# Running maxima from score copies in SBUF, GpSimd's arithmetic on VectorE, and new tables of rounds in a gated mix of attention and a gated FFN

## The chip, the core and the metric

The kernel runs on one core of one Trainium2 chip. The metric is the device time of one execution in microseconds (us); a program's time is the median over its runs. The core's engines run side by side, each through its own instructions in order: TensorE (PE, with its weight loads as PEld), VectorE (DVE), ScalarE (ACT), GpSimd (POOL) and SyncE (SP, which here only issues DMAs). They wait for each other through semaphores. SBUF is the working memory of 128 partitions, PSUM holds the outputs of matmuls.

## What is computed

```python
def _A_ref(x, wqkv, wo):                       # 16 heads of 28, 2048 tokens, D = 448
    qkv = (x @ wqkv).reshape(B, S, 3, H, Dh).transpose(2, 0, 3, 1, 4)
    q, k, v = qkv[0], qkv[1], qkv[2]
    scores = jnp.einsum("bhqd,bhkd->bhqk", q, k) * (Dh ** -0.5)
    p = _softmax(scores, axis=-1)
    o = jnp.einsum("bhqk,bhkd->bhqd", p, v)
    return o.transpose(0, 2, 1, 3).reshape(B, S, D) @ wo

def _B_ref(x, W_gate, W_up, W_down):           # F = 1792
    gate = x @ W_gate
    up = x @ W_up
    gate = gate * (gate > 0)
    return (gate * up) @ W_down

g = _sigmoid((A_x * gate_w).sum(-1, keepdims=True))
out = g * _A_ref(A_x, A_wqkv, A_wo) + (1 - g) * _B_ref(A_x, B_W_gate, B_W_up, B_W_down)
```

## The kernel before

**Precision.** Operands of the projections and of the FFN are split into a high part (ScalarE's copy to a rounded type, `act_high`) and a low part (the difference, `low` on VectorE or `pool_low` on GpSimd), and each product is a sum of 11 terms (`TERMS`) over chunks of 128 rows.

**Three stages.** First come the projections of Q, K and V, whose results go to DRAM (`qk_d`) through GpSimd's DMA queue. Then come 32 rounds, two for each head. Last come the rest of the gate/up units, the down projection and the output projection. The change lies in the rounds and at the border to them.

**One round.** Round `v` works on head `v // 2` and half of the keys. A "visit" has 16 pairs of score matmuls (`score`, K against Q, 128 keys x 512 queries twice, into one PSUM tile of 1024 columns). 12 of the 16 pairs go through ScalarE's exp straight into the probability tiles `P` (`done`): for the first three blocks of queries the maximum is already folded into the matmul through two extra rows of Q. The four pairs of the last block of queries are raw: ScalarE copies them to SBUF (L262), VectorE keeps a running maximum (`block_max`, L228, tile `rm`) that reads them in PSUM, GpSimd reduces it over the partitions (`all_max`, L234), VectorE subtracts it from 2048 columns at a time (`take_max`, L239), and ScalarE takes the exp (`take_exp`, L246). A round's second half rescales the head's sum where the maximum of its two visits differs (`rescale`). At the end of a round the PV product (`pv`, tile `po`, L601) runs as 64 matmuls in two halves without a pause.

Beside the scores a round holds 12 pairs of "maxima" matmuls (`smax`, tile `sm`, L169), which compute the next heads' row maxima for the folded rows; VectorE reduces each pair (L171), and `smax_end` turns them over and stores them into Q's extra rows. And it holds the gate/up matmuls of the FFN (`gu_mm`, L547), 11 for each half of a unit of 128 hidden columns; `relu` and `spill_h` take them away, and a DMA stores them. In the first rounds ScalarE and GpSimd also split the gate/up weights (`split_f`, L103 and L112), 14 units in all, which then go to DRAM and are loaded again for later token blocks.

**What sets the order.** No scheduler: each engine's order is the order in which the code records instructions, and the four strings `FIRST`, `LONG`, `WIDE` and `LATE` set it within a round. One letter is one step: `s` a pair of scores, `m` a pair of maxima with its reduction, `x` one gate/up matmul, `A` the all-reduce, `d` a subtraction, `e` an exp of 2048 columns, `n` the end of a head's maxima, `w` the split of weights, `c` and `f` the rescaling, `P` and `Q` the halves of the PV product, `u` and `l` leftovers of the projections. `LONG` has 33 `x`, `WIDE` 44, `LATE` no `m`. `AHEAD = 3` of a visit's pairs are issued in the round before. Score pairs and maxima pairs take turns in three PSUM tiles (`ps_w`): a pair waits until the pair three before it has been read. `small_things` issues a head's loads and the division by the row sums at the start of a round and at its eighth `s`: at the start of an even round `load_k` and `load_q` for two heads on, at the eighth `s` `row_sums` and `spread` (a reciprocal, its store, and four loads back that wait for the store).

## Time and profile before

| | us |
|---|---|
| median of 3 runs | 1289.12 (1284.76 to 1290.27) |
| the profiled execution: time | 1281.88 |
| the profiled execution: span of its trace | 1280.1 |
| busy in the span: PE, PEld | 1241.6 (97%), 872.5 (68%) |
| busy in the span: DVE, ACT, POOL | 962.1 (75%), 776.1 (61%), 191.2 (15%) |

Ends of matmuls are modelled and overlap with the next ones, so PE's 97% is no measure of how well it is used; the times from one PV block to the next are. In a row of the trace the columns are start, duration, engine, line, operation, output<-inputs, shape and count, and in brackets the idle time before it with the engine that ended it. `PEclk` is the granted clock of TensorE (1.00 is full speed).

### The profile page before, as it was taken

How to read it: one execution, taken by the hardware profiler on the slowest of the kernel's cores; microseconds unless marked ns; L12 is line 12 of the kernel's file. 1: busy time of each engine (PE TensorE's matmuls, PEld its weight loads, DVE VectorE, ACT ScalarE, POOL GpSimd, SP SyncE). 2: the span in 40 equal slices, each digit the busy share in tenths (PEclk: the TensorE clock that was granted, in tenths of full speed). 3: DMA queues.
4: the chain of work that ended last, by engine and by line, in shares of the span. 5: the costliest groups of instructions: out<-in, count | busy, mean ns of one | idle time of the engine just before them, and what ended most of it. 6: DMA issues, size and time to landing. Idle time of an engine off the chain costs nothing.

```text
span 1280.1 us, 16867 instructions
## 1 busy us (share of the span) xinstructions
PE 1241.6 (97%) x6431; PEld 872.5 (68%) x6431; DVE 962.1 (75%) x1022; ACT 776.1 (61%) x894; POOL 191.2 (15%) x188
## 2 busy tenths in 40 slices
PE   9999699999999999999999999999999999999998
PEld 6888466665656666666666566666666566799998
DVE  6466679898988989998988889898989543563342
ACT  5223377777877677777777677767777784122121
POOL 4222221221221000000000001000000010551020
PEclk9999899999999999999999999999999999999999
DMA  9845275352626543342536243342442325745432
GB/s 323 289 189 222 84 209 117 127 163 72 169 76 201 169 121 84 103 133 64 163 104 186 81 113 103 84 130 93 132 128 76 119 90 195 228 147 159 132 115 80
DMA packets 64269, 178.37 MB, mean 139 GB/s; under 512 B 13730, under 2 KB 20578, under 8 KB 59554
## 3 DMA queue, kind: packets, MB, share of 16 engines
q1 hardware_dynamic: 57452, 151.00, 39.5%
q0 software_dynamic: 6304, 25.82, 5.3%
q8 instruction: 51, 0.84, 0.3%
q10 hardware_dynamic: 432, 0.46, 0.1%
q14 instruction: 30, 0.25, 0.1%
HBM read 118.58 MB, written 58.87 MB: 139 GB/s over the span
## 4 chain that ended last, share of the span: by engine, by line
PE 89%; DVE 4%; ACT 2%; DMA 2%; issue 1%; POOL 1%; SPq 0%; POOLq 0%; ACTq 0%
PE gu L547 19%; PE s L256 19%; PE po L601 18%; PE sm L169 13%; PE acc L808 10%; PE qk L381 5%; DVE rm L228 3%; PE wo L767 3%; PE v L399 3%; ACT P L262 1%; DVE mx L171 1%; DMA wg<-ws_d 1%; DMA or<-o_d 0%; DMA wr<-wq 0%; ACT P L260 0%
## 5 line engine op out<-in xcount | busy, mean ns | idle before, releaser
L171 DVE TENSOR_REDUCE mx<-sm 128x1 f32<-128x1024 f32 x384 | 456.5, 1219 | 60.6 <-PE sm L169 59.5
L547 PE MATMUL gu<-X,wg 128*128 128x512 f32 x1232 | 373.9, 398 | 10.8 <-POOL wg L112 7.2
L260 ACT ACTIVATE P<-s 128x1024 f32<-128x1024 f32 x306 | 306.7, 1025 | 116.8 <-PE s L256 113.1
L256 PE MATMUL s<-Q,K 128*128 128x512 f32 x1024 | 319.5, 403 | 13.6 <-DVE rm L228 11.2
L547 PEld LDWEIGHTS gu<-X,wg 128*128 128x128 f32 x1232 | 231.6, 189 | 69.1 <-POOL wg L112 7.6
L256 PEld LDWEIGHTS s<-Q,K 128*128 128x128 f32 x1024 | 184.7, 189 | 99.3 <-DVE rm L228 10.9
L169 PE MATMUL sm<-K,Q 128*128 128x512 f32 x768 | 243.2, 398 | 7.5 <-DVE mx L171 3.6
L601 PE MATMUL po<-P,V 128*32 128x512 f32 x1640 | 227.3, 594 | 0.0
L228 DVE TENSOR_TENSOR rm<-s,rm 128x512 f32<-128x512 f32 x218 | 150.4, 690 | 74.6 <-ACT P L262 57.3
L169 PEld LDWEIGHTS sm<-K,Q 128*128 128x128 f32 x768 | 137.1, 188 | 52.6 <-ACT P L260 10.1
L234 POOL PARTITION_ALL_REDUCE rm<-rm x32 | 57.2, 1788 | 673.7 <-DVE rm L228 618.8
L601 PEld LDWEIGHTS po<-P,V 128*32 128x32 f32 x1640 | 62.6, 110 | 116.2 <-issue 111.5
L808 PE MATMUL acc<-WD,hh 128*128 128x448 f32 x672 | 138.5, 365 | 0.0
L262 ACT ACTIVATE P<-s 128x1024 f32<-128x1024 f32 x104 | 105.1, 1024 | 46.6 <-PE s L256 45.4
L808 PEld LDWEIGHTS acc<-WD,hh 128*128 128x128 f32 x672 | 126.2, 188 | 10.4
L239 DVE TENSOR_TENSOR P<-P,rm 128x2048 f32<-128x2048 f32 x52 | 117.9, 2272 | 5.8 <-POOL rm L234 5.8
L601 PE MATMUL po<-V 128*32 128x512 f32 x408 | 115.0, 594 | 0.0
L103 ACT ACTIVATE hh<-hr 128x512 fp32r<-128x512 f32 x56 | 35.2, 631 | 117.8 <-PE acc L808 113.8
L246 ACT ACTIVATE P<-P 128x2048 f32<-128x2048 f32 x52 | 99.4, 1914 | 5.3 <-DVE P L239 4.5
L260 ACT ACTIVATE V<-s 128x1024 f32<-128x1024 f32 x78 | 78.9, 1025 | 37.1 <-PE s L256 35.2
L109 DVE TENSOR_TENSOR hh<-hr,hh 128x512 fp32r<-128x512 f32 x56 | 49.4, 883 | 62.2 <-ACT hh L103 62.2
L381 PE MATMUL qk<-X,W 128*128 128x512 f32 x308 | 77.4, 398 | 0.3 <-DVE X L109 0.2
(79 smaller groups left out, 772.4 us busy)
## 6 DMA issues: line engine op xcount, KB each, us to landing
wg<-ws_d SPq DMA_DIRECT2D x42, 896.0 KB
K<-qk_d SPq DMA_DIRECT2D x64, 224.0 KB
Q<-qk_d SPq DMA_DIRECT2D x64, 224.0 KB
h_d<-h SPq DMA_DIRECT2D x56, 256.0 KB
hr<-h_d SPq DMA_DIRECT2D x56, 256.0 KB
ws_d<-wg SPq DMA_DIRECT2D x14, 896.0 KB
qk_d<-st POOLq DMA_DIRECT2D x21, 512.0 KB, 3.2
wgr<-wgu SPq DMA_DIRECT2D x13, 512.0 KB
```

Of the source, the lines that this page charges most:

```text
L169: nc.tensor.matmul(ps[:, c, :], Q[h][:, u * P:(u + 1) * P], K[h % 3][:, k0:k0 + TB], start=True, stop=True)
L171: nc.vector.tensor_reduce(MX[h][:, 2 * u + half:2 * u + half + 1], ps, axis=AX.XY, op=OP.max)
L228: nc.vector.tensor_tensor(r, x, y, op=OP.max)
L239: nc.vector.tensor_tensor(QUAD[q], QUAD[q], RM[v, b].unsqueeze(1).to_broadcast([P, 4, TB]), op=OP.subtract)
L246: nc.scalar.activation(q, q, AF.Exp, scale=SCALE)
L256: nc.tensor.matmul(ps[:, c], K[h % 3][:, k * P:(k + 1) * P], Q[h][:, j * TB:(j + 1) * TB], start=True, stop=True)
L260: nc.scalar.activation(dst, ps, AF.Exp, scale=SCALE)
L262: nc.scalar.activation(dst, ps, AF.Copy)
L381: nc.tensor.matmul(ps, W[:, a, c * P:(c + 1) * P], xf(tb, b), start=(n == 0), stop=(n == NT - 1))
L547: nc.tensor.matmul(ps, WS[i][:, s, a], xf(i // NF, b), start=(n == 0), stop=(n == NT - 1))
L601: nc.tensor.matmul(po[32 * j:32 * j + 32], V[:, h // 4 % 2, k, h % 4], AT.pop((v, k, j)), start=(k == k0), stop=(k == k0 + NK // 2 - 1))
L808: nc.tensor.matmul(ACC[i // NF][t][:, :D], HH[i][:, a, t * P:(t + 1) * P], WD[:, f, b], start=(f == 0 and n == 0), stop=(f == NF - 1 and n ...
```

## The change

- `block_max` becomes `block_min` on a step of its own, `b`: ScalarE copies a raw pair to SBUF with its sign turned, and VectorE takes the minimum of whole pairs (128x1024, both inputs in SBUF) into a tile `r2`: three such operations a visit, then one minimum of its two halves and one turn of the sign (with the maximum of the earlier visit, in the second half), both 128x512. No instruction but ScalarE's copy reads a raw pair in PSUM.
- `take_max` adds the negated maximum on VectorE (step `g`); the exp gets a negative scale. A way by DMA (step `d`) stands in the code, but no string has the letter.
- The low parts of the gate/up weights go from GpSimd to VectorE in all 28 halves.
- `AHEAD = 4`: all four raw pairs are issued in the round before.
- A first all-reduce of a small tile stands right at the program's start.
- `load_k` and `load_q` move behind `row_sums` and `spread`, and these from a round's eighth `s` to its tenth. The zero rows of the third Q buffer come by DMA from another Q buffer, not from a GpSimd memset.
- New strings, with the same counts of `m` and `x` (`FIRST` has one `s` more), and `WIDE` at other rounds.

```diff
-AHEAD = 3
+AHEAD = 4
-FIRST = "AmxmxsmxmxxlxsxumsmmmxxxsxdxxxsxssmxxmxsmmxdexxsxsewsPQ"
-LONG = "ssmnAxxxxsmsxmxsmxxxmsmxxxsmxxmxsdxsxxxsxsmxxxsmxxmexxsmxxdxxcsxsefwsPQ"
+FIRST = "mmbslmxusbssmsxbxsxmxxsmxxmmsxxsxsAxgbxsmsbxxxxmmxegmxxbxxPweQ"
+LONG = "AnsmsxxxxsxxssxgmxxxxsmsxxsxssgxmxsxxmsmxxxmsmxxxxscmxsxemxxxbxxsmxbmbPefwQ"
...
-        if k % (NK // 2):
-            parts = [(p[:, c], r) for c in range(2)]
-        elif v % 2:
-            parts = [(p[:, 0], RM[v - 1, b]), (p[:, 1], r)]
-        else:
-            parts = [(p[:, 0], q[:, 1])]
-        for x, y in parts:
-            nc.vector.tensor_tensor(r, x, y, op=OP.max)
...
+        if (v, b) not in R2:
+            R2[v, b] = att.tile([P, 2, TB], F32, name=f"r2_{v}_{b}", tag="r2", bufs=1)
+            left[v, b] = NK // 4 - 2
+            nc.vector.tensor_tensor(R2[v, b], todo_max.pop(0)[2], todo_max.pop(0)[2], op=OP.min)
+            return
+        nc.vector.tensor_tensor(R2[v, b], R2[v, b], todo_max.pop(0)[2], op=OP.min)
...
+        nc.vector.tensor_tensor(r, r2[:, 0], r2[:, 1], op=OP.min)
+        if v % 2:
+            nc.vector.scalar_tensor_tensor(r, r, -1.0, RM[v - 1, b], op0=OP.mult, op1=OP.max)
+        else:
+            nc.vector.tensor_scalar(r, r, -1.0, None, op0=OP.mult)
...
-        nc.vector.tensor_tensor(QUAD[q], QUAD[q], RM[v, b].unsqueeze(1).to_broadcast([P, 4, TB]), op=OP.subtract)
+            nc.vector.tensor_tensor(QUAD[q], QUAD[q], m, op=OP.add)
...
-            nc.scalar.activation(dst, ps, AF.Copy)
+            nc.scalar.activation(dst, ps, AF.Copy, scale=-1.0)
+            todo_max.append((v, chunks[0][1], dst))
...
+        nc.gpsimd.partition_all_reduce(warm_r, warm_r, P, bass_isa.ReduceOp.max)
...
-        if q == 0 and h and h + 2 < H:
-            load_k(h + 2)
-            load_q(h + 2)
...
             row_sums(h - 1)
             spread(h - 1)
+            if h + 2 < H:
+                load_k(h + 2)
+                load_q(h + 2)
...
-                if ns == 8:
+                if ns == 10:
                     small_things(2 * v + 1)
...
-                    split_f(parts // 2, act_high, pool_low, (parts % 2,))
+                    split_f(parts // 2, act_high, low, (parts % 2,))
...
-                nc.gpsimd.memset(f32(QS[2])[96:128], 0.0)
+                for a, b in ((GD, 12), (GD + 12, 4)):
+                    nc.sync.dma_start(f32(QS[2])[a:a + b].rearrange("p j t -> p (j t)"), Q[1][GD + 2:GD + 2 + b].bitcast(F32))
```

Three places show how the order of instructions moves. VectorE around the end of a round in the second half of the rounds, before the change (`sm` are maxima pairs, `s` score pairs in PSUM, `os` the head's output):

```order
L228 TENSOR_TENSOR rm_6653<-s_8_3_6649,rm_6653 128x512
L228 TENSOR_TENSOR rm_6653<-s_10_3_6659,rm_6653 128x512 x2
L228 TENSOR_TENSOR rm_6653<-s_12_3_6666,rm_6653 128x512 x2
L627 TENSOR_TENSOR os_6235<-os_6235,rb_6571 128x512
L228 TENSOR_TENSOR rm_6653<-s_14_3_6712,rm_6653 128x512 x2
L171 TENSOR_REDUCE mx_6722<-sm_6723 128x1
```

And the end of an early round with the change (`r` is the tile of pairwise minima, `wg` the split weights):

```order
L222 TENSOR_TENSOR r_3_0_1794<-r_3_0_1794,V 128x1024
L228 TENSOR_TENSOR rm_0_1820<-r_3_0_1794 128x512
L230 SCALAR_TENSOR_TENSOR rm_0_1820<-rm_0_1820,rm_0_1574 128x512
L109 TENSOR_TENSOR wg_1841<-wgr_1367,wg_1841 128x384 x2
L109 TENSOR_TENSOR wg_1841<-wgr_1367,wg_1841 64x2x128
L109 TENSOR_TENSOR wg_1852<-wgr_1606,wg_1852 128x384 x2
L109 TENSOR_TENSOR wg_1852<-wgr_1606,wg_1852 64x2x128
L634 TENSOR_TENSOR os_1386<-os_1386,rb_1705 128x512
L109 TENSOR_TENSOR mh_1897<-mr_1896,mh_1897 16x128
L171 TENSOR_REDUCE mx_1911<-sm_1912 128x1
```

The maximum of a round's last raw pair stood between the output and the next round's first reduction; now the whole chain is closed before the round's end, and in early rounds two units of weights follow it.

GpSimd at its first all-reduce of the rounds, before the change (`ISA` without operands loads code for the next operation; `pair` holds the first unit's raw weights):

```order
L112 TENSOR_TENSOR wg_1145<-pair,wg_1145 128x384
L234 ISA
L234 ISA rm_1150<-rm_1150 128x512
L388 DMA qk_d<-pair 128x2x512
L112 ISA
L112 TENSOR_TENSOR wg_1145<-pair,wg_1145 128x384
L112 TENSOR_TENSOR wg_1145<-pair,wg_1145 64x2x128
L716 MEMSET Q_1200 32x2048
```

With the change:

```order
L411 DMA v_d_79<-V 128x512
L392 DMA qk_d<-pair 128x2x512
L238 ISA rm_0_1218<-rm_0_1218 128x512
L175 MEMSET m_1315 128x4
L238 ISA rm_0_1321<-rm_0_1321 128x512
```

The low parts, the memset of Q and both loads of code are gone from this place; a load of code stands at the program's start.

SP's queue over an even round, before the change (`ls` and `l_d` are the row sums, `rb` their spread, `h_d` a stored hidden tile):

```order
L611 DMA ls_6471<-os_6235 128x1x16
L148 DMA K_103<-qk_d 28x2048 x4
L153 DMA Q_106<-Q_106 2x2048
L155 DMA Q_106<-qk_d 28x2048 x4
L617 DMA l_d_90<-rq_6568 128x16
L623 DMA rb_6571<-l_d_90 32x512 x4
```

With the change:

```order
L618 DMA ls_6461<-os_6230 128x1x16
L573 DMA h_d_6510<-h_6508 128x512
L546 DMA wg_6512<-ws_d_2367 128x1792
L624 DMA l_d_90<-rq_6540 128x16
L630 DMA rb_6543<-l_d_90 32x512 x4
L148 DMA K_103<-qk_d 28x2048 x4
L153 DMA Q_106<-Q_106 2x2048
L155 DMA Q_106<-qk_d 28x2048 x4
```

The eight loads of K and Q pass from the head of the round to behind the store of the reciprocal and the four loads that wait for it.

More of the change, by code (lines that the diff above doesn't have):

```diff
@@ L245, in take_exp, with score @@
         q = QUAD[q].rearrange("p c t -> p (c t)")
-        nc.scalar.activation(q, q, AF.Exp, scale=SCALE)
-    def score(late=True):
+        nc.scalar.activation(q, q, AF.Exp, scale=-SCALE)
+    def score():
         v, done, q, half, chunks = stream.pop(0)
@@ L423, in gated_mix_kernel @@
         nc.vector.memset(warm, 0.0)
+        warm_r = pa.tile([P, 16], F32, name="warm_r")
+        nc.vector.memset(warm_r, 0.0)
         ps = ps_x("warm_ps")
@@ L495, in gated_mix_kernel @@
                 m += 1
-            news = [(score, False) for back in EARLY if back == len(mixed) - n]
+            news = [(score,) for back in EARLY if back == len(mixed) - n]
             for k, c in enumerate(news):
@@ L654, in small_things @@
             spread(h - 1)
+            if h + 2 < H:
+                load_k(h + 2)
+                load_q(h + 2)
         if h and q == 2:
             normalise(h - 1)
-    split_f(0, act_high, pool_low, (0,))
+    split_f(0, act_high, low, (0,))
     fetch_f(1)
-    while todo_max:
-        block_max(*todo_max.pop(0))
     for v, (order, nu) in enumerate(ROUNDS):
@@ L722, in gated_mix_kernel @@
                 pv(v, "PQ".index(o))
-        left = [k for k in todo_exp + todo_sub + todo_all if k[0] == v]
-        assert not passes and not left and v not in PO or len(stream) == max(0, 16 * (2 * H - 1 - v) - AHEAD), (v, passes, left, len(stream) + 16 * (v + 1))
+        rest = [k for k in todo_exp + todo_sub + todo_all if k[0] == v]
+        assert not passes and not rest and v not in PO or len(stream) == max(0, 16 * (2 * H - 1 - v) - AHEAD), (v, passes, rest, len(stream) + 16 * (v + 1))
     assert not stream and m == len(maxima), (len(stream), m)
```

49 lines of the change are left out of this document (25 added, 24 removed).

## The prediction

> **What bounds the kernel now.** I read the shares of the chain of waits first, then the busy time by stretches, then the chain in order of time, then the rows around two places where TensorE stops.
>
> ```profile
> PE 89%; DVE 4%; ACT 2%; DMA 2%; issue 1%; POOL 1%; SPq 0%; POOLq 0%; ACTq 0%
> ...
> 128.00:160.00 32.00, 20.50 (x72) 14.36 (x71) 21.87 (x21) 10.37 (x16) 9.20 (x10) 0.84 0.23 84
> 192.00:320.00 128.00, 125.50 (x678) 81.15 (x680) 113.85 (x114) 99.40 (x113) 24.45 (x24) 1.00 0.42 120
> 832.00:960.00 128.00, 126.19 (x669) 82.97 (x668) 114.26 (x116) 92.69 (x95) 7.22 (x6) 1.00 0.41 121
> ```
>
> TensorE holds 89% of the chain. In the stretches (columns: length, PE, PEld, DVE, ACT, POOL busy, clock) it is busy 125 to 126 us of 128, and VectorE 114 of 128: the rounds run close to both. Only 128 to 160 us, where the first round starts, is loose: 20.5 us of 32 and a granted clock of 0.84.
>
> ```profile
> 318.29 7.00 PE po L601 x64
> 344.68 0.94 PE gu L547 x4
> 347.23 7.00 PE po L601 x64
> ```
>
> A LONG round lasts 347.23 - 318.29 = 28.94 us. Its work: 16 score pairs, 12 maxima pairs and 33 gate/up matmuls are 89 matmuls at 0.94/4 = 0.235 us, 20.9 us, plus the PV block, 7.0 us: 27.9. About 1.0 us of a round is lost, and this is where:
>
> ```profile
> 325.23 1.20 PE L256 MATMUL s<-Q,K 128*128 128x512 f32 x4
> 326.69 0.70 PE L169 MATMUL sm<-K,Q 128*128 128x512 f32 x2 [0.27 <-DVE rm L228]
> 326.92 1.02 ACT L260 ACTIVATE P<-s 128x1024 f32<-128x1024 f32 x1
> 327.06 1.41 DVE L228 TENSOR_TENSOR rm<-s,rm 128x512 f32<-128x512 f32 x2
> 327.24 1.10 PE L547 MATMUL gu<-X,wg 128*128 128x512 f32 x4
> 328.62 0.70 PE L256 MATMUL s<-Q,K 128*128 128x512 f32 x2 [0.28 <-DVE rm L228]
> 329.15 0.62 PE L169 MATMUL sm<-K,Q 128*128 128x512 f32 x2
> 347.16 5.36 PE L601 MATMUL po<-P,V 128*32 128x512 f32 x48
> ```
>
> From 325.23 to 329.15 twelve matmuls, worth 2.82 us, take 3.92: 1.1 lost. From there to 347.16 it is 77 matmuls in 18.0 us, worth 18.1: nothing lost. Both stops wait for the running maximum on VectorE, which reads the scores out of PSUM and so holds one of the three PSUM tiles past ScalarE's copy. That is the whole loss of a steady round, and the most that a steady round can win.
>
> ```profile
> 135.48 0.63 PE L256 MATMUL s<-Q,K 128*128 128x512 f32 x2
> 136.40 5.02 DVE L228 TENSOR_TENSOR rm<-P,rm 128x512 f32<-128x512 f32 x6
> 137.06 0.51 ACT L103 ACTIVATE wg<-pair 128x384 fp32r<-128x384 f32 x1
> 142.61 1.07 PE L169 MATMUL sm<-K,Q 128*128 128x512 f32 x2 [3.32 <-DVE mx L171]
> 144.76 1.48 PE L547 MATMUL gu<-X,wg 128*128 128x512 f32 x3
> 156.04 1.78 POOL L112 TENSOR_TENSOR wg<-pair,wg 128x384 fp32r<-128x384 f32 x2 [8.01 <-issue]
> 157.87 0.79 PE L547 MATMUL gu<-X,wg 128*128 128x512 f32 x1 [7.18 <-POOL wg L112]
> 170.32 7.24 PE po L601 x64
> ```
>
> The first round stops twice: 3.32 us behind seven maxima in a row on VectorE, 7.18 us behind a low part on GpSimd, which itself stands 8.01 us without a visible wait after GpSimd's first all-reduce. After each, TensorE is slow: three matmuls take 1.48 us.
>
> **The change, part by part.** VectorE's prices:
>
> ```profile
> L171 DVE TENSOR_REDUCE mx<-sm 128x1 f32<-128x1024 f32 x384 | 456.5, 1219 | 60.6 <-PE sm L169 59.5
> L228 DVE TENSOR_TENSOR rm<-s,rm 128x512 f32<-128x512 f32 x218 | 150.4, 690 | 74.6 <-ACT P L262 57.3
> L239 DVE TENSOR_TENSOR P<-P,rm 128x2048 f32<-128x2048 f32 x52 | 117.9, 2272 | 5.8 <-POOL rm L234 5.8
> L246 ACT ACTIVATE P<-P 128x2048 f32<-128x2048 f32 x52 | 99.4, 1914 | 5.3 <-DVE P L239 4.5
> L627 DVE TENSOR_TENSOR os<-os,rb 128x512 f32<-128x512 f32 x16 | 11.6, 724 | 0.0
> L109 DVE TENSOR_TENSOR X<-xr,X 128x1024 fp32r<-128x1024 f32 x6 | 7.3, 1224 | 3.6 <-ACT X L103 3.5
> L109 DVE TENSOR_TENSOR W<-wr,W 128x336 fp32r<-128x336 f32 x6 | 2.8, 504 | 2.0 <-ACT W L103 1.9
> L109 DVE TENSOR_TENSOR W<-wr,W 64x224 fp32r<-64x224 f32 x2 | 0.8, 390 | 0.1
> ```
>
> *Running maxima from SBUF.* Per visit out go 7 or 8 operations of 0.69 (5.2 us on the mean), in come three of 128x1024 and two of 128x512: 3 x 1.224 + 2 x 0.724 = 5.1. VectorE gains nothing; what is gained is that a raw score's PSUM tile is free after ScalarE's 1.02 us. I walked a new LONG round by hand: 0.47 us a pair on PE, 1.02 a copy or exp, 1.22 a reduction, three tiles in turn, 0.2 us from producer to consumer as between the rows above. Its start "s m s xxxx s xx s s" runs without a stop if VectorE is free within 2.0 us of the PV block's end (the fifth pair, wanted at 3.3, needs the first reduction done). The later stops are small, 0.2 to 0.3 each behind the second subtraction, 0.5 in all. So 1.1 lost becomes 0.5: **-0.6 a round, -17 over 28 LONG and WIDE rounds**. Bounds: -1.1 (nothing lost, -31) and 0 (the loss only moves).
>
> *Subtraction at later places.* Still two of 2.27 a round; adding the negated maximum costs what subtracting did. Both exps follow early enough: in the walk the second subtraction ends near 10.5 us, the PV block starts at 21.5, its second half at 25. Nothing.
>
> *Low parts on VectorE.* Fourteen units at 2 x 0.55 (384 elements, between the rows of 336 and 512) plus 0.4 for the 64-row tail (256 elements, the row of 224): 1.5 a unit, 21 us. They stand at the ends of the first eight rounds, one or two units each, behind the last minimum. VectorE ends that chain about when PV ends in the walk, so one unit plus the 0.7 of the output sum puts the next round's start 2.0 to 2.6 late, two units 3.5 to 4.1. Past 2.0 the fifth pair waits: 0.35, 0.7, 0.4, 0.9, 0.35, 2.2, 0.35, 0.8 over the eight boundaries, **+6**. Bounds: 0 (back-to-back operations overlap, as 1.41 for two of 0.69 does not yet show) and +12 (every unit in full over the 28.9 us rounds, less the 1 us of slack each has).
>
> A rule against just this: the Trainium skill's Perfetto Trace Analysis, under Optimizing Scalar/DVE Operations, says that GpSimd and VectorE share an SBUF read port, so that shifting work between them may not help. By it some of the 21 us was already paid as waiting, and the term would be nearer 0 than 6; no row here separates the two.
>
> *First round.* In GpSimd's order no low part follows an all-reduce any more, and a first all-reduce is done at the very start, so the 8.01 us has no place here. VectorE then sets this round. Before the second PV half it owes 11 reductions (13.4), the first visit's five operations (5.1), two minima of the next (2.45), two subtractions (4.54), the first unit's low parts, the last projection's low part and the gates (1.5 + 0.69 + 0.6), after 1.6 us of waiting for ScalarE's first high part (137.57): 29.85; then an exp, 2.1 with its hand-over, and half a PV block, 3.5: 35.5 us from 135.95, where the last score pair of the projections ends. Now it ends at 177.56, 41.6 us after: **-6**. Bounds: -9 (overlap) and -2 (VectorE idles 4 us between tiles).
>
> The clock belongs to this term: 0.84 in the first round's stretch, with matmuls at twice their time after stops of 3.32 and 7.18 us. My longest new stops are 2.2 and 2.5. The Trainium skill's TensorE: Matmul & The Clock Gate, Part 1, puts the halving after an idle window of about 3.4 us; the trace agrees, with its two stops. By that rule the new stops leave the clock alone; were both to halve it, an estimate from that page's 3.4 us is 2 x 1.7 us more.
>
> *The all-reduce at the start* pushes GpSimd's memsets and its first store of projections back by up to some 10 us, the 8.01 and the operation itself; three staging tiles and two halves of K's third buffer take five stores before a reuse, so 0 to +1. *The zero rows of Q by DMA* wait for VectorE's low part, where a GpSimd memset stood behind the 8.01 us: nothing. *Four pairs ahead* moves one pair from a round's start into the round before: in the walk above.
>
> *Loads of K and Q in mid round.* They pass from the head of an even round to behind the row sums' round trip on SP; the first user is the second matmul pair of the next round.
>
> ```profile
> 330.25 2.71 SPq L148 DMA_DIRECT2D K<-qk_d  x4
> 339.82 0.35 SPq L617 DMA_DIRECT2D l_d<-rq  x1
> 348.15 2.69 SPq L623 DMA_DIRECT2D rb<-l_d  x4
> 346.00:348.00 2.00, 2.00 (x14) 0.96 (x16) 2.00 (x2) 1.89 (x3) 0.00 (x0) 1.00 0.09 26
> 561.46 1.72 SPq L148 DMA_DIRECT2D K<-qk_d  x4
> 570.00:572.00 2.00, 2.00 (x10) 1.60 (x10) 2.00 (x3) 1.03 (x1) 0.00 (x0) 1.00 0.80 172
> 573.55 0.32 SPq L617 DMA_DIRECT2D l_d<-rq  x1
> 576.89 1.71 SPq L623 DMA_DIRECT2D rb<-l_d  x4
> ```
>
> K and Q took from 561.46 to about 572 with the queues busy, 10.5 us. New: the reciprocal at some 9.2 us into the round, 3.3 to the spread's issue, 1.7 for it, then 10.5: landed at 25, wanted at 29. Nothing, with 4 us to spare; queued behind it are the hidden tile's store and the next weights, wanted a round later.
>
> **Sum.** -17 + 6 - 6 = -17 us: a span of 1263 against 1280.1, 1265 against the profiled execution's own 1281.88. That execution lies below the three runs shown (1284.76 to 1290.27); against their median, 1289.12, the forecast is **1272**, its own range 1258 to 1281.
>
> **Rivals.**
> (1) *Only the first round wins.* The 1.1 us moves to the dense stretch "s m s m" after the second subtraction. For it: VectorE is busy 114 of 128 now and gets no relief. Against: the old rounds, as dense, lose nothing after 329.15. 1289 - 6 = 1283.
> (2) *Slower: VectorE becomes the bound.* Place: the round's end, where three minima, two 512s and the last reductions stand in one piece. If VectorE comes to the first reduction later than 2.0 us after PV in every round, not in eight, each round stops there. At 3.3 us the stop is 1.3, and with 0.5 within the round the loss is 1.8 against 1.1: +0.7 x 28 = +20, with -6 from the first round 1303. For it: an odd round carries four more 512-element operations (rescaling, normalising, output sum), 2.9 us at 0.724; with 12 reductions, two subtractions and the 5.1 that is 27.1 before the hidden products, in a round of 28. Against: it ends its chain before PV's end in my walk.
> (3) *Slower: K and Q land late.* The old spread waited 8.3 us (339.82 to 348.15) in a round with weight stores in the queue. With that and a slow drain (K issued at 330.25, the queues busy until 346) they land at 36, 7 us after their first use. In rounds 2, 4, 6 and 8: +28, and some 6 for a slowed clock: 1289 - 17 + 34 = 1306; in all thirteen loads over 1360. Against: the 8.3 us was spent behind K and Q themselves, which now come after.
>
> **Chances.** Forecast 0.60, (1) 0.14, (2) 0.16, (3) 0.10. The range, 1257 to 1300, holds the forecast, rival (1) and most of what (2) can cost. Half a per cent, 6.4 us, is about what can be told from no change: the forecast lies beyond it but for 0.03, half of (1) does, and 0.02 of each of (2) and (3) ends within it. Faster 0.61, same 0.17, slower 0.22.
>
> **What would show it.** Right: PV block to PV block 28.3 to 28.5 us in the second half and no wait of TensorE's scores for running maxima; the first PV block ending near 171 us with a clock above 0.84 before it; some longer rounds before 430 us. Wrong: rounds of 29 us or more after 450 us with waits for mx (rival 2), waits of sm for K or Q at the head of odd rounds (rival 3), or an idle GpSimd of 8 us still in the first round.

## The result, and the profile after

The changed kernel takes 1270.32 us (median of 4 runs, 1269.59 to 1270.41), the kernel before 1287.33 in the runs beside it: a ratio of 0.9866, 95% interval 0.984 to 0.9891. The forecast was 1272. The span of the profiled execution is 1268.6 us, against 1280.1 before.

The shares of the chain of waits and the busy time by stretches (length, PE, PEld, DVE, ACT, POOL busy, clock, DMA share, GB/s) of the changed kernel, as they were shown of the kernel before:

```profile
PE 86%; DVE 6%; ACT 3%; DMA 3%; issue 1%; POOL 1%; SPq 0%; ACTq 0%; DVEq 0%; POOLq 0%
...
128.00:160.00 32.00, 25.44 (x98) 16.94 (x96) 24.88 (x28) 21.58 (x28) 4.39 (x6) 1.00 0.61 168
192.00:320.00 128.00, 124.93 (x697) 77.72 (x697) 122.93 (x125) 96.24 (x115) 9.74 (x7) 1.00 0.40 120
320.00:448.00 128.00, 124.30 (x660) 80.50 (x659) 118.24 (x118) 93.11 (x103) 9.36 (x8) 1.00 0.46 146
832.00:960.00 128.00, 128.00 (x713) 80.39 (x713) 116.35 (x110) 92.00 (x97) 10.87 (x8) 1.00 0.39 113
960.00:1088.00 128.00, 119.41 (x636) 78.64 (x635) 59.55 (x64) 76.14 (x83) 11.49 (x7) 0.97 0.41 138
```

Two of these stretches in the kernel before:

```profile
320.00:448.00 128.00, 125.55 (x693) 79.09 (x686) 114.94 (x120) 94.81 (x107) 23.61 (x23) 1.00 0.52 154
960.00:1088.00 128.00, 125.87 (x702) 80.42 (x700) 74.47 (x85) 90.48 (x95) 10.19 (x8) 1.00 0.36 120
```

Four stages went four ways. The first round gained 5 us of TensorE's time in 128:160 and kept its clock at 1.00. The late rounds are full: 128.00 of 128. The early ones, 192 to 448, are no fuller than before, with VectorE now at 122.93 of 128. And 960:1088, which held 125.87 us before, holds 119.41 at a lower clock: something new is lost there.

Where a round begins and ends is read off TensorE's timeline, from the end of one PV block to the end of the next. By that, with the rounds numbered from 0:

| stretch | before, us | after, us | difference |
|---|---|---|---|
| to the end of the first PV block | 177.56 | 171.28 | -6.3 |
| rounds 1 to 8 (one WIDE more after) | 234.46 | 240.21 | +5.7 |
| rounds 9 to 28 (one WIDE fewer after) | 587.18 | 569.39 | -17.8 |
| rounds 29 to 31 (LATE) | 74.50 | 81.98 | +7.5 |
| rest | 206.40 | 205.74 | -0.7 |
| span | 1280.1 | 1268.6 | -11.5 |

A WIDE round is 2.1 to 2.3 us longer than a LONG one, so at equal work the early rounds lost 3.4 and the later ones won 15.6: the changed kernel's LONG rounds from 9 on last 28.21 to 28.28 us each. The start of one of them on PE and DVE, after a PV block that ends at 526.77:

```profile
526.74 0.71 PE L264 MATMUL s<-Q,K 128*128 128x512 f32 x2
527.29 0.63 PE L169 MATMUL sm<-K,Q 128*128 128x512 f32 x2
527.76 0.62 PE L264 MATMUL s<-Q,K 128*128 128x512 f32 x2
527.96 0.28 DVE L109 TENSOR_TENSOR mh<-mr,mh 16x128 fp32r<-16x128 f32 x1 [1.78 <-ACT mh L185]
528.17 1.21 DVE L171 TENSOR_REDUCE mx<-sm 128x1 f32<-128x1024 f32 x1
...
529.15 0.62 PE L264 MATMUL s<-Q,K 128*128 128x512 f32 x2
529.30 2.27 DVE L247 TENSOR_TENSOR P<-P,rm 128x2048 f32<-128x2048 f32 x1
...
530.08 1.09 PE L264 MATMUL s<-Q,K 128*128 128x512 f32 x4
```

No row of PE carries a wait in brackets. VectorE waits 1.78 us for ScalarE's copy of the transposed maxima, makes their low part and begins its reductions (528.17); no maximum of raw scores stands ahead of them. An early round, number 4, starts otherwise:

```profile
259.02 2.20 POOL L238 PARTITION_ALL_REDUCE rm<-rm  x1 [28.36 <-DVE rm L232]
259.60 3.72 DVE L109 TENSOR_TENSOR wg<-wgr,wg 128x384 fp32r<-128x384 f32 x6
263.35 0.69 DVE L616 TENSOR_TENSOR os<-po,os 128x512 f32<-128x512 f32 x1
263.96 1.21 DVE L171 TENSOR_REDUCE mx<-sm 128x1 f32<-128x1024 f32 x1
265.23 1.19 PE L264 MATMUL s<-Q,K 128*128 128x512 f32 x4 [1.75 <-DVE mx L171]
```

The PV block ends at 260.02; two units' low parts hold VectorE until 263.3, the first reduction ends at 265.17, and the round's fifth pair (its fourth of scores) waits 1.75 us for it. This is the stop that the prediction described. One thing in it the prediction did not have: GpSimd's all-reduce (259.02) runs beside the first low part, which alone of the six is slow, 1.28 us where the same operation takes 0.55 without the all-reduce (below).

The loss in LATE is in round 29:

```profile
997.19 0.27 PE L181 MATMUL mt<-ident,m 128*16 128x128 f32 x1
999.05 1.16 SPq L188 DMA_DIRECT2D Q<-mh  x2
1003.86 2.90 PE L264 MATMUL s<-Q,K 128*128 128x512 f32 x6 [6.40 <-DMA Q<-mh]
...
1006.76 8.20 PE po L608 x64
```

The new LATE has its `n`, which transposes the last head's maxima and sends them into Q, ahead of the round's last seven letters; LONG and the old LATE have it second. The next scores read that Q, so TensorE waits for a transpose, three copies and a DMA: 6.40 us. After it a PV block takes 8.20 us instead of 7.00, and the stretch's clock is 0.97. The round takes 34.08 us where it took 24.98.

### The profile page after: what moved, and what is told of

Same layout as the page of the kernel before. It is cut to its first block, busy times and chain, and to the rows that moved or that the text cites. A ratio compares the mean times of both kernels' runs of the same rounds, so it can differ in the third digit from the quotient of the medians.

```text
span 1268.6 us, 16622 instructions
## 1 busy us (share of the span) xinstructions
PE 1238.7 (98%) x6431; PEld 865.4 (68%) x6431; DVE 973.5 (77%) x985; ACT 765.0 (60%) x894; POOL 159.2 (13%) x146
## 4 chain that ended last, share of the span: by engine, by line
PE 86%; DVE 6%; ACT 3%; DMA 3%; issue 1%; POOL 1%; SPq 0%; ACTq 0%; DVEq 0%; POOLq 0%
PE gu L554 19%; PE s L264 18%; PE po L608 16%; PE sm L169 13%; PE acc L816 10%; PE qk L385 5%; PE wo L775 3%; PE v L403 3%; DVE mx L171 2%; ACT P L268 1%; DVE wg L109 1%; DVE P L247 1%; ACT P L254 1%; DVE r L222 1%; DMA wg<-ws_d 1%
## 5 line engine op out<-in xcount | busy, mean ns | idle before, releaser
L554 PE MATMUL gu<-X,wg 128*128 128x512 f32 x1232 | 366.8, 395 | 2.2 <-DMA wg<-ws_d 2.2
L268 ACT ACTIVATE P<-s 128x1024 f32<-128x1024 f32 x306 | 295.1, 1025 | 94.3 <-PE s L264 92.6
L169 PEld LDWEIGHTS sm<-K,Q 128*128 128x128 f32 x768 | 134.1, 188 | 55.7 <-DVE mx L171 13.2
L238 POOL PARTITION_ALL_REDUCE rm<-rm x32 | 66.5, 2079 | 832.2 <-DVE rm L230 415.3
L270 ACT ACTIVATE P<-s 128x1024 f32<-128x1024 f32 x104 | 105.9, 1026 | 52.9 <-PE s L264 50.3
L268 ACT ACTIVATE V<-s 128x1024 f32<-128x1024 f32 x78 | 76.3, 1026 | 22.1 <-PE s L264 21.6
L567 DVE TENSOR_TENSOR h<-gu,rl 128x512 f32<-128x512 f32 x56 | 38.2, 681 | 42.9 <-ACT rl L564 21.7
```

The lines of the kernel that those rows point to most:

```text
L169: nc.tensor.matmul(ps[:, c, :], Q[h][:, u * P:(u + 1) * P], K[h % 3][:, k0:k0 + TB], start=True, stop=True)
L238: nc.gpsimd.partition_all_reduce(RM[v, b], RM[v, b], P, bass_isa.ReduceOp.max)
L268: nc.scalar.activation(dst, ps, AF.Exp, scale=SCALE)
L270: nc.scalar.activation(dst, ps, AF.Copy, scale=-1.0)
L554: nc.tensor.matmul(ps, WS[i][:, s, a], xf(i // NF, b), start=(n == 0), stop=(n == NT - 1))
```

## The experiments

### The letter n

```diff
-LATE = "xssxbxxxbxsAxsgxxgxsxxxsxxxsxxxsxsexxsxxwxsxxxxxxsxxxxcxxxsxxxxxxfnesbssPQ"
+LATE = "xssnxbxxxbxsAxsgxxgxsxxxsxxxsxxxsxsexxsxxwxsxxxxxxsxxxxcxxxsxxxxxxfesbssPQ"
```

> The changed kernel with one letter of LATE moved: the transposed maxima of the last head (n) come after the third letter instead of before the last six. Theory: in the changed kernel the scores of round 29's end wait 6.40 us for Q<-mh and TensorE then runs its next PV block in 8.20 us instead of 7.00, so both go: the last PV block of the rounds ends 7 to 8.5 us earlier, the span is 1260 to 1262 against 1268.6, about 1262 us timed. Rival: the 8.3 us that rounds 29 to 31 lost came from the other new places in LATE (the letters b, g, A), and the wait only shows where they end: then under 3 us are won, 1266 to 1269.

Measured: span 1261.7, 1263.47 us in the profiled run, a median of 1265.23 over 4 runs (1262.71 to 1268.34); a ratio to the kernel before of 0.9842, interval 0.9811 to 0.9873. Round 29 takes 24.99 us, so 9.1 of its 34.08 went. The span fell by 6.9 only, since the stretch behind the rounds took 1.9 more: there TensorE stops for weights in every profile, and its clock was 0.58 in the 4 us after the stop here, 1.00 in the changed kernel (more in the last section). No wait for Q<-mh is left. The other letters of LATE cost nothing: its three rounds now take 72.9 us, 1.6 less than before the change. This version has the lowest median of the study.

### What the steady rounds won by: maxima from SBUF alone

```diff
-            job = (v, chunks[0][1], chunks[0][0], ps if late else dst, dst)
+            job = (v, chunks[0][1], chunks[0][0], dst, dst)
```

> The kernel before, with only one edit: its running maxima read the copies of the raw scores in SBUF, at the same places and in the same number and size, instead of the scores in PSUM. Theory: what held TensorE in a steady round was the PSUM tile kept by VectorE past ScalarE's copy, so the waits of scores for rm go, and a LONG round shortens by 0.6 to 1.1 us, from 28.95 to 27.9 to 28.35: 17 to 30 us over 28 rounds, a span of 1250 to 1263 against 1280.1. Rival: VectorE's work at the round's start is the limit and the wait only changes its name (from rm to mx): rounds stay within 0.2 us, a span of 1275 to 1284; the gain of the changed kernel's steady rounds then came from its new order.

Measured: span 1287.6, ratio 1.0041 (1.0028 to 1.0054). The theory, which was the prediction's, falls: most LONG rounds from 9 on stay at 28.6 to 28.95 us (rounds 9, 15 and 21, of 29.8 to 29.9, are told of below with the tiles). The start of one on PE, ACT and DVE:

```profile
537.82 1.02 ACT L262 ACTIVATE V<-s 128x1024 f32<-128x1024 f32 x1
...
538.88 1.42 DVE L228 TENSOR_TENSOR rm<-V,rm 128x512 f32<-128x512 f32 x2 [2.27 <-ACT V L262]
...
540.21 1.22 DVE L171 TENSOR_REDUCE mx<-sm 128x1 f32<-128x1024 f32 x1
...
541.49 0.73 PE L256 MATMUL s<-Q,K 128*128 128x512 f32 x2 [0.58 <-DVE mx L171]
```

The stop for a PSUM tile held by rm is gone, but VectorE stands 2.27 us for the copy of the fourth raw pair, its maximum comes first in the queue, and the reductions behind it are late by that: the wait changes its name. So the rival is right about the steady rounds. The span lies above its 1275 to 1284 because the run also lost in rounds 1, 3, 4, 6 and 8. Why it lost there, the groups of two windows show (192 to 320 us, where GpSimd makes low parts, then 448 to 704, where it makes none):

```profile
L228 DVE TENSOR_TENSOR rm<-P,rm 128x512 f32<-128x512 f32 x22 | 18.4, 837 | 5.7 <-ACT P L262 5.2
...
L228 DVE TENSOR_TENSOR rm<-P,rm 128x512 f32<-128x512 f32 x45 | 31.1, 690 | 13.0 <-ACT P L262 11.0 <-DVE rm L228 0.5
```

The same maximum takes 0.837 us beside GpSimd's subtractions and 0.690 without them. In the kernel before, where it reads PSUM, the same two windows have 0.689 and 0.690. The Trainium skill's SBUF — State Buffer, under "SBUF: two separate sides", says that a VectorE operation with two SBUF inputs and a GpSimd operation that reads SBUF exclude each other; the rows agree, and GpSimd's own subtractions there take 1.211 us on the mean instead of 1.026.

### Four pairs ahead alone

```diff
-AHEAD = 3
+AHEAD = 4
-LONG = "ssmnAxxxxsmsxmx...efwsPQ"
+LONG = "smnAxxxxsmsxmx...efwssPQ"
```

(and so in the other three strings)

> The kernel before, with one thing of the change: four score pairs ahead instead of three. In each of its four strings the first s goes to the end, ahead of P, so that no raw pair is left at a round's start; the maxima still read PSUM. Theory, after the run with maxima from SBUF: VectorE does nothing for 2.27 us at the head of a round, because the first thing in its queue is the maximum of the fourth raw pair, which waits for ScalarE's copy; the reductions behind it come late, and TensorE stops once or twice. With four ahead that maximum stands under the PV block: a LONG round goes from 28.95 to 28.2 to 28.4, the twenty rounds from the tenth on lose 11 to 15 us, the span is 1262 to 1269 against 1280.1 and 1283.7. Rival: the raw pair's maximum holds its PSUM tile at the round's end as it did at the start, and the gain of the changed kernel comes from pairs of 1024 elements that are put later: then the rounds stay within 0.2 us.

Measured: span 1364.2, ratio 1.057 (1.0535 to 1.0604). This theory falls too: most LONG rounds take 30.7 to 30.8 us, and some 32 to 34. The end of one:

```profile
583.14 2.28 DVE L239 TENSOR_TENSOR V<-V,rm 128x2048 f32<-128x2048 f32 x1
...
586.25 0.69 DVE L228 TENSOR_TENSOR rm<-s,P 128x512 f32<-128x512 f32 x1
586.99 0.73 PE L256 MATMUL s<-Q,K 128*128 128x512 f32 x2 [2.50 <-DVE rm L228]
```

Several raw pairs now stand together ahead of the PV block. Their maxima are behind a subtraction of 2.28 us in VectorE's queue and read PSUM, so that the tiles stay taken, the last pair waits 2.50 us, and the PV block behind it too.

### Both together

> The kernel before with two things of the change together: four score pairs ahead (as in the run that did this alone) and maxima that read the copies in SBUF (as in the run that did that alone). Theory: each needs the other. Four ahead alone takes 30.77 us a LONG round, because at the round's end the maxima of the raw pairs stand behind a subtraction in VectorE's queue and hold two PSUM tiles that long (a stop of 2.50 us); copies in SBUF alone leave it at 28.9, because the fourth raw pair's maximum stands ahead of the reductions at a round's start. Together neither stop is there: a LONG round from the tenth on takes 28.1 to 28.5 us. Rounds 1 to 8 stay longer by 3 to 8 us in all, since GpSimd's low parts slow maxima from SBUF. Span 1264 to 1274. Rival: the places of b, g and A in the new strings are what wins; then the LONG round stays at 28.8 or above and the span at 1280 or above.

The edit is the sum of the last two. Measured: span 1288.3, ratio 1.0052 (1.0037 to 1.0068), and LONG rounds of 28.12 to 28.23 us from 11 on (15 and 21 apart), as short as the changed kernel's, with the old strings but for one letter moved. The end of the PV block that ends at 540.9:

```profile
537.30 3.62 PE L601 MATMUL po<-P,V 128*32 128x512 f32 x32
537.69 2.94 DVE L228 TENSOR_TENSOR rm<-V,rm 128x512 f32<-128x512 f32 x4
...
540.81 2.08 POOL L234 PARTITION_ALL_REDUCE rm<-rm  x1 [25.99 <-DVE rm L228]
540.85 0.73 PE L256 MATMUL s<-Q,K 128*128 128x512 f32 x2
```

The maxima of all four raw pairs are done under the PV block, which needs nothing of VectorE, and the copies have freed the tiles. The span was outside the expected 1264 to 1274 because rounds 1, 3, 6 and 8 lost more than the 3 to 8 us allowed (low parts on GpSimd, as above), and the old WIDE and rounds 9, 15 and 21 are long (the tiles, below). So the LONG round's 0.7 us is settled by four runs:

| LONG round, us | three ahead | four ahead |
|---|---|---|
| maxima read PSUM | 28.93 (before) | 30.77 |
| maxima read SBUF | 28.86 | 28.20 |

Neither edit wins alone.

### The changed kernel with three ahead

```diff
-AHEAD = 4
+AHEAD = 3
-LONG = "AnsmsxxxxsxxssxgmxxxxsmsxxsxssgxmxsxxmsmxxxmsmxxxxscmxsxemxxxbxxsmxbmbPefwQ"
+LONG = "sbAnsmsxxxxsxxssxgmxxxxsmsxxsxssgxmxsxxmsmxxxmsmxxxxscmxsxemxxxbxxmxbmPefwQ"
```

(and so in the other three strings; the first minimum of a visit waits until two copies are there)

> The changed kernel with three score pairs ahead: the last s of each string and its minimum (the last b) go to the start of the next round, ahead of A; the minima still read the copies in SBUF. Theory: the minimum of the fourth pair again waits for ScalarE's copy at the head of VectorE's queue, with the reductions behind it, and a LONG round from the tenth on takes 28.7 to 29.0 us instead of 28.25: 9 to 15 us over twenty rounds, a span of 1277 to 1285. Rival: pairwise minima from SBUF and the later subtractions are what wins, and three ahead costs under 3 us, a span of 1268 to 1272.

Measured: span 1330.6, ratio 1.0347 (1.0331 to 1.0363); all rounds from 1 to 28 take 30.6 to 31.1 us.

```profile
606.09 1.23 DVE L224 TENSOR_TENSOR r<-r,P 128x1024 f32<-128x1024 f32 x1 [4.48 <-ACT P L272]
...
608.89 1.21 DVE L171 TENSOR_REDUCE mx<-sm 128x1 f32<-128x1024 f32 x1
608.94 1.78 POOL L240 PARTITION_ALL_REDUCE rm<-rm  x1 [29.28 <-DVE rm L232]
610.15 1.20 PE L266 MATMUL s<-Q,K 128*128 128x512 f32 x4 [1.45 <-DVE mx L171]
```

VectorE idles 4.48 us for the fourth pair's copy, and the all-reduce and the first reduction come behind its minimum. The direction is the theory's, the size, 2.7 us a LONG round, three to six times its. A likely reason, which no run tests, is that the new strings take the subtraction at the sixteenth letter of LONG, where the old ones had it at the thirty-fourth, and can wait for the all-reduce far less.

### Low parts back on GpSimd

```diff
-                    split_f(parts // 2, act_high, low, (parts % 2,))
+                    split_f(parts // 2, act_high, pool_low, (parts % 2,))
```

> The changed kernel with the low parts of step w on GpSimd, as before the change (the first weight unit's stay on VectorE). Rounds 1 to 8 of the changed kernel lose 9.6 us against its steady ones (28.25 a LONG, 30.5 a WIDE round). Theory: the low parts on VectorE are that loss, but on GpSimd they slow VectorE's minima from SBUF, as the run with maxima from SBUF showed (0.80 to 0.96 us instead of 0.69 while GpSimd subtracts), and GpSimd's next all-reduce, at a round's start, waits behind them: the rounds 1 to 8 come out between 4 us shorter and 10 us longer, more likely longer, a span of 1265 to 1279. Rival: VectorE's 21 us were the whole price, and without them the early rounds are as the late ones: a span of 1259 to 1262.

Measured: span 1312.0, ratio 1.0217 (1.0199 to 1.0234): longer than the theory's worst. Rounds 1 to 8 take 283.3 us instead of 240.2.

```profile
340.69 7.50 POOL L112 TENSOR_TENSOR wg<-wgr,wg 128x384 fp32r<-128x384 f32 x6 [22.78 <-ACT wg L103]
...
341.05 1.74 DVE L222 TENSOR_TENSOR r<-r,P 128x1024 f32<-128x1024 f32 x1
...
342.82 1.38 DVE L228 TENSOR_TENSOR rm<-r 128x512 f32<-128x512 f32 x1
...
355.90 1.80 POOL L238 PARTITION_ALL_REDUCE rm<-rm  x1 [7.71 <-issue]
357.74 2.29 DVE L247 TENSOR_TENSOR P<-P,rm 128x2048 f32<-128x2048 f32 x1 [9.31 <-POOL rm L238]
361.22 1.22 PE L264 MATMUL s<-Q,K 128*128 128x512 f32 x2 [8.98 <-DVE mx L171]
```

Both halves of the theory are there: minima that took 1.22 and 0.69 us take 1.74 and 1.38 beside GpSimd, and the all-reduce waits behind the low parts. What was under-priced is a third thing: 5.9 to 7.7 us in which GpSimd stands whenever an all-reduce follows subtractions. Here it is 7.71 us, with the all-reduce's input ready since 345.07, so nothing that the profile shows held it. VectorE's subtraction waits 9.31 us for it, and TensorE 8.98. The Trainium skill's GPSIMD Engine Reference, under "Instruction dispatch", gives about 6 us for loading a kernel's code; the gaps here were 5.9 to 7.7 after low parts.

### The first round's part, on the kernel before

One weight unit's low parts on VectorE, and the all-reduce at the start:

```diff
-    split_f(0, act_high, pool_low, (0,))
+    split_f(0, act_high, low, (0,))
...
+        nc.gpsimd.partition_all_reduce(warm_r, warm_r, P, bass_isa.ReduceOp.max)
```

(and so for the unit's other half, in step `u`)

> The kernel before, with only the first round's part of the change: a first all-reduce of GpSimd at the start and the first weight unit's low parts on VectorE; all later low parts stay on GpSimd, the order of every round stays. Theory: the 8.01 us in which GpSimd stood and the 7.18 us in which TensorE waited for its low part were the loss, so the first PV block ends 5 to 8 us earlier (171 instead of 177.5) and the span is 1272 to 1275. Rival: VectorE's seven maxima in a row and the order of the first round set its length; the wait turns into one for VectorE, and under 2 us are won.

Measured: span 1278.1, ratio 0.9945 (0.9924 to 0.9965); the first PV block ends at 172.37, 5.1 us earlier than 177.5. The theory holds for the first round. The span lies above its 1272 to 1275, which were reckoned from the profile of 1280.1; against the second profile of the kernel before (1283.7, below) it is 5.6 less. The stop of 7.18 us is gone. One behind VectorE's maxima, 5.02 us at 145.1, is left, which the changed kernel's order doesn't have.

### The changed kernel without the all-reduce at the start

> The changed kernel without the all-reduce at the start. In the changed kernel GpSimd stands 9.65 us ahead of that first all-reduce. Theory: GpSimd stands some 8 us at its first all-reduce wherever that is, so the one of the first round ends 8 us later; the first subtractions and exps of the round follow it, with VectorE's queue behind the first of them, and the first PV block ends 3 to 8 us later than 171.3; the span is 1271 to 1277. Rival: VectorE alone sets the first round, as the prediction's sum had it, and the all-reduce has the time to spare: under 1 us of difference.

Measured: 1271.2 us (1270.03 to 1272.09), span 1270.3. The first PV block ends at 171.36 instead of 171.28: the rival was right. The first round's all-reduce and its input, with the early one, then without it:

```profile
148.66 0.43 DVE L232 TENSOR_SCALAR rm<-rm 128x512 f32<-128x512 f32 x1
149.26 1.79 POOL L238 PARTITION_ALL_REDUCE rm<-rm  x1 [5.93 <-DMA Q<-Q]
```
```profile
148.72 0.43 DVE L232 TENSOR_SCALAR rm<-rm 128x512 f32<-128x512 f32 x1
149.37 1.81 POOL L238 PARTITION_ALL_REDUCE rm<-rm  x1 [5.97 <-DMA Q<-Q]
```

GpSimd is idle for 5.9 us ahead of it either way. The brackets name a DMA, but the all-reduce starts 0.2 us after VectorE's last operation on its input has ended: it waited for VectorE, which sets this round, and an early all-reduce has nothing to win in it. Whether GpSimd would have stood there on its own account, as it does after subtractions, these two runs can't show, since the wait for VectorE would hide it.

### All low parts on VectorE, on the kernel before

All three calls of `split_f` take `low` instead of `pool_low`.

> The kernel before with all low parts of the weights on VectorE, and nothing else. Theory: the first round wins what it won with only its own unit there, 5 us; rounds 1 to 8 take VectorE's 21 us more, where it is busy 114 us of 128 and its maxima stand at the rounds' ends and starts: 4 to 12 us are lost, the eight rounds take 238 to 247 us instead of 234.5, the span is 1278 to 1292. Rival: the low parts find VectorE's idle time, or free it of a contention with GpSimd: the eight rounds take 234 to 236 us and the span is 1275 to 1279.

Measured: span 1279.3, ratio 0.9982 (0.9968 to 0.9995). The first PV block ends at 171.49, 6.0 us earlier, without any early all-reduce. Rounds 1 to 8 take 238.0 us instead of 234.5: the low parts that VectorE makes there, 16.9 us of its busy time in two groups, cost 3.5. The theory holds, at the low end of its bounds. The larger group in rounds 1 to 8 of the changed kernel, then here:

```profile
L109 DVE TENSOR_TENSOR wg<-wgr,wg 128x384 fp32r<-128x384 f32 x25 | 18.3, 770 | 0.3
```
```profile
L109 DVE TENSOR_TENSOR wg<-wgr,wg 128x384 fp32r<-128x384 f32 x23 | 11.8, 553 | 0.2
```

The same operation takes 0.770 us on the mean there and 0.553 here. In the changed kernel the last minimum, which starts GpSimd's all-reduce, stands just ahead of the low parts, and at the ends of rounds 1 to 7 the one low part that runs beside the all-reduce takes 1.28 to 1.40 us; the others take 0.55. Here no low part meets an all-reduce, and none is slow.

### Low parts evened out

```diff
-            elif o == "w":
+            elif o in "wW":
...
+                if o == "W":
+                    ready = parts + 2 if ready == parts + 4 else parts
```

(LONG and WIDE have the `W` six letters behind their second `g`)

> The changed kernel with n moved as in the first run, and the low parts evened out: where four halves of weight units are due in one round (as at the ends of rounds 2, 3, 5 and 7), two of them are split already in the middle of the round, not all at its end. Theory: rounds 4 and 6, 2.8 and 3.8 us over a steady round, come from two units in one piece ahead of the next round's first reduction; half of that goes, 2 to 5 us in all, a span of 1257 to 1260 against 1261.7. Rival: VectorE is full there (122.9 of 128 us), so that the loss only moves into the rounds in which the units now stand: 0 to 2 us more, 1261 to 1264.

Measured: span 1264.7, 1266.35 us, ratio 0.9856 (0.9831 to 0.9881), against 1261.7 with `n` moved alone. Rounds 4 and 6 shorten by 2.0 and 3.2 us, round 8 by 1.3, and rounds 2, 3, 5 and 7, where the units now stand, lengthen by 2.1, 1.6, 2.1 and 3.6. The rival was right, the loss a little over its bound: VectorE is full, and the place of the work only chooses the round that pays. Round 6 owes part of its 3.2 to something else: a stop of 1.11 us at a PSUM tile (below), which this build doesn't have.

### The loads of K and Q back at the head of even rounds

```diff
+        if q == 0 and h and h + 2 < H:
+            load_k(h + 2)
+            load_q(h + 2)
...
-            if h + 2 < H:
-                load_k(h + 2)
-                load_q(h + 2)
```

> The changed kernel with the loads of K and Q at the head of even rounds again, ahead of the row sums, instead of behind them in mid round. Theory: the loads have time to spare in both places (no wait of TensorE for K or Q in the trace of the changed kernel, the last one issued 9 us ahead of its round): under 1 us of difference in every round, a span of 1267 to 1270. Rival: at a round's head they hold up the queue for the row sums and weight stores, and a round in which that happens is longer by 1 us or more: 1272 or above.

Measured: span 1285.8, ratio 1.0039 (1.0026 to 1.0052), 17.2 us more than the changed kernel. The time seemed to speak for the rival, but the trace doesn't. Of 17.1 us in the rounds, 14.6 stand in five, 7, 13, 15, 19 and 25, while every even round from 8 on is as long as in the changed kernel. Round 13, PE:

```profile
535.65 1.20 PE L264 MATMUL s<-Q,K 128*128 128x512 f32 x4 [0.65 <-ACT P L268]
...
540.74 0.73 PE L264 MATMUL s<-Q,K 128*128 128x512 f32 x2 [0.66 <-ACT P L268]
541.32 0.63 PE L554 MATMUL gu<-X,wg 128*128 128x512 f32 x2
542.59 0.73 PE L264 MATMUL s<-Q,K 128*128 128x512 f32 x2 [0.65 <-ACT P L268]
```

Scores wait for ScalarE's copy of the scores just before them, as if there were one PSUM tile and not three. Read out of the two built programs, the PSUM banks of round 13's scores (s) and maxima (m), in order, the changed kernel's first:

```
s4 m2 s6 s4 s2 s6 m4 s2 m6 s4 s2 s6 s4 m2 s6 m4 ...
s2 m4 s6 s2 s2 s6 m2 s4 m6 s4 s4 s6 s2 m4 s6 m2 ...
```

The pool's choice of a tile isn't a strict turn, so a pair doesn't always wait for the pair three before it, as the description of the kernel and the prediction's walk have it. With the loads elsewhere it gave the same bank twice running, twice in this round (s2 s2, s4 s4), and so in rounds 19 and 25 (3.4 to 3.5 us more in each of the three), and once in 7 and 15 (2.5 and 1.7). The changed kernel has one such repeat in all, in its round 6, the longest of its early LONG rounds; the kernel before has three, in rounds 5, 11 and 23, the three LONG rounds of 29.7 us; both together (four ahead, from SBUF) has them in 9, 15, 17 and 21, of which the LONG ones, 9, 15 and 21, took 30.1, and maxima from SBUF alone has the same four (29.8 to 29.9). A repeat doesn't always cost: the changed kernel with three ahead has one in each of rounds 1, 4, 10, 16, 22 and 28, and these take 30.6 to 30.9 us, no longer than the rounds around them (30.8 to 31.1). No run changed the bank alone, so this is read from programs and traces that agree, not shown by itself.

### The kernel before once more

> The kernel before, unchanged. Its three first runs were 1284.76 to 1290.27 us while its profiled execution took 1281.88. One theory: the runs scatter by 0.4% because some waits of this kernel fall out differently each time, and the profiled execution was at the low end: the new profile's span lies elsewhere in 1280 to 1289, with another sum of waits in the rounds. The other: profiled executions are always the faster ones by some 5 us for this kernel: the new span is again within 1 us of 1280.

Measured: span 1283.7 and 1285.45 us in the profiled run, a median of 1285.48 over 10 (1283.01 to 1287.76). The 25 runs beside the last four experiments had a median of 1285.37 (1281.8 to 1288.54). The first theory holds: the execution that the prediction was made on, 1281.88, lay at the low end. Of its 3.6 us more, 1.9 stand in round 9, which waited twice for X:

```profile
427.66 0.50 PE L547 MATMUL gu<-X,wg 128*128 128x512 f32 x1 [1.51 <-DMA X<-x_d]
...
1091.43 6.95 PE L547 MATMUL gu<-X,wg 128*128 128x512 f32 x22 [2.87 <-DMA wg<-ws_d]
```

The rest, 1.7, follows the last round: a wait of 2.87 us for weights, after which 22 matmuls take 6.95 us. In the first profile the wait was 2.77 and the matmuls took 5.42.

## Why the prediction was right, and where it was not

The number, 1272 against 1270.32, and the sign were right; of the steps some were. That the number fits so closely is luck: a loss that the sum didn't have (LATE, 7.5 us) and one that it had too small (the low parts, 3.7) were met by a base that lay some 5.5 us low and by steady rounds a little better than forecast.

- **Steady rounds, -0.6 each, 28.35 us: mis-sized only.** 28.25 was measured, 0.69 under the 28.93 of before; TensorE is busy 128.00 of 128 in 832:960 and in the three windows of 128 us ahead of it. **The reason given was half of one.** "What is gained is that a raw score's PSUM tile is free after ScalarE's 1.02 us" is worth 0.07 alone; and four pairs ahead, which the prediction named in one clause as part of its walk, costs 1.8 alone and is the other half.
- **Low parts on VectorE, +6.** On the kernel before they cost 3.5. In the changed kernel rounds 1 to 8 are 9.7 us over its own steady rounds (28.25, WIDE 30.5), by boundary 0.6, 0.8, 0.4, 2.8, 0, 3.8, 0 and 1.3, where 0.35, 0.7, 0.4, 0.9, 0.35, 2.2, 0.35 and 0.8 were predicted: the places right, the boundaries ahead of rounds 4 and 6 too small. The sum took 0.55 us for a 384-element low part throughout and didn't have the all-reduce beside them, 0.5 to 0.85 us on one of them at each boundary. By an estimate from round 4's rows the stop of 1.75 us would be 1.0 without it. Of round 6's 3.8, 1.57 us is the stop behind the low parts and 1.11 the one at its repeated bank, where a maxima pair waits for ScalarE's exp of the scores just before it.
- **The Trainium skill's rule on the shared port** (Perfetto Trace Analysis). It was weighed as a reason for a term nearer 0 than 6. It is real, but it struck elsewhere: low parts beside the all-reduce (1.28 us instead of 0.55) were not thought of; maxima that read PSUM were never slowed (0.689), so moving the low parts freed nothing in the kernel before; minima from SBUF are slowed by low parts on GpSimd. Of the 43 us that leaving them there costs in rounds 1 to 8, most is the all-reduce behind them, for which VectorE waits 38.9 us between 192 and 448 us.
- **First round, -6:** -6.3, by the way described: VectorE sets it, 35.2 us from the last score pair of the projections (136.10) to the PV block's end, where 35.5 were predicted, the longest stop 2.12 us, the clock 1.00. The all-reduce at the start, priced at 0 to +1, has no part in it.
- **K and Q in mid round, nothing:** no wait for K or Q is in the trace, and rival (3) fell. Leaving the loads in place would still have cost 17 us, most likely by way of the banks, which no step of the prediction looked at.
- **LATE: the step that is missing.** The part on the change walks a LONG round and says nothing of the new LATE. Its `n` cost 9.1 us in round 29; LATE as a whole lost 7.5, since its other letters won 1.6. The strings had it to be read: a transposition with its DMA, two letters ahead of scores that read what it writes.
- **The base.** The sum was made against an execution at the low end. Against the second profile of the kernel before, 1283.7, the change is worth 15.1 us, against 1280.1 it is 11.5. The median moved by 17.0 because the runs of before lie, at the median, 5.5 us above their first profiled execution and those of after don't. So the predicted 17 was met by a gain of 11.5 on the base it was worked from.
- **The clock.** The prediction held that stops of 2.2 and 2.5 us would leave it alone. In the first round they did (longest 2.12, clock 1.00). Behind the rounds a stop of that length is sometimes followed by a slow clock, whatever the kernel (last section), so the argument is weaker than it looks.
- **The chances** don't follow from their own terms: forecast 0.60 less 0.03, and half of rival (1)'s 0.14, make 0.64 for faster and leave 0.14 for the same, not 0.61 and 0.17.

Rival (1) fell, since the steady rounds won. Of rival (2), VectorE as the bound, the mechanism came true in rounds 1 to 8 alone.

## What to carry to other kernels

Ask of a buffer that is freed earlier what stands first in the queue of the engine that waited: here the tile and the place of its last pair had to change together, and each alone was worth nothing or did harm. Walk every kind of round that an edit rewrites, the rare ones too: three of 32 rounds gave back 7.5 us, and moving one letter took 9.1 off them. And where a pool chooses tiles, compare the chosen tiles of two builds ahead of blaming a wait on what was moved.

## What the runs showed of the hardware that was not expected

- A 128x512 maximum on VectorE takes 0.690 us, from PSUM or from SBUF. Beside GpSimd's subtractions it takes 0.80 to 0.96 on the mean from SBUF (maxima from SBUF alone) and 0.689 from PSUM (the kernel before), and a 128x512 minimum of two SBUF tiles 1.301 instead of 0.692 (low parts back on GpSimd).
- GpSimd's all-reduce slows VectorE too: a 128x384 subtraction of two SBUF tiles takes 1.03 to 1.40 us beside it and 0.55 otherwise, at the ends of rounds 0 to 7 of the changed kernel.
- GpSimd stands 5.9 to 7.7 us ahead of an all-reduce that follows subtractions, in the kernel before as well as with the low parts back on GpSimd. Where no subtractions come before it, the all-reduce starts 0.1 to 0.2 us after its input.
- Behind the rounds TensorE stops for weights in every profile. After stops of 2.16, 2.35, 2.64, 2.65, 2.87, 2.90, 3.05 and 3.66 us the clock over the next 4 us was 0.50 to 0.63, after stops of 2.19, 2.41, 2.50, 2.56, 2.77 and 3.07 us it was 1.00, so the length alone doesn't decide. One such slow spell is worth some 1.5 us: 22 matmuls took 6.95 us after the stop of 2.87 and 5.42 after that of 2.77. After the stop of 6.40 a PV block took 8.20 instead of 7.00.
